# Two layers of memory attention and FNet on one core: rows of q and k by a direct transfer, a narrower memory update, and a new written order

## The chip, the core and the metric

The kernel runs on one core of a Trainium2 chip. The metric is the device time of one execution in microseconds. The core has five instruction streams that matter here: PE (matrix multiplies, with PEld for its weight loads), DVE, ACT and POOL (elementwise work), and SP (which issues the DMA transfers). PE's results land in PSUM; the other data lie in SBUF or DRAM.

## What is computed

The input x has 2048 rows of 512. Two layers are applied, each with an attention with memory (A) and a Fourier mixing (B); every step adds to a residual and starts from a layer norm without weights. Both layers use the same weights.

```python
# A, per head (H = 32 heads of 16), over N = 4 segments of L = 512 rows
for s in range(N):
    logits = einsum("bhqd,bhkd->bhqk", qs, ks) * scale + mask   # causal
    a_dot = softmax(logits) @ vs
    a_mem = (phi(qs) @ M) / (phi(qs) @ z + 1e-6)                # phi(t) = t+1 or exp(t)
    outs.append(g * a_mem + (1 - g) * a_dot)
    M = M + phi(ks)^T @ vs;  z = z + sum(phi(ks))
x = x + concat(outs) @ wo
# B
y = dft_seq_re @ (x @ dft_hid_re.T) - dft_seq_im @ (x @ dft_hid_im.T)
x = x + y
```

## The kernel before, in words

**Groups.** The attention is cut into 32 groups: two layers, four segments, and in each segment four groups of 8 heads. A group is numbered i. For each group `s_p` (line 784) projects q and k: the layer-normed rows stand transposed in a tile `g`, the weights in tiles `w`, both as a pair of 16-bit numbers (a high and a low part), so that each product is three matmuls `b<-g,w 128x512`. `t_split` (line 681) then splits the result in PSUM again into a high and a low half, in a tile that it calls `hl` (printed as `w`), and brings it to the row buffers `qst` and `kst`, in which the two halves lie on neighbouring partitions, so that one matmul of 48 rows gives the sum of three products. In the kernel before that goes by DRAM: two writes `d<-w` of 128 KB in all, and four reads `qst<-d` or `kst<-d`. There are two sets of row buffers (NR = 2), so the reads of group i wait until group i-2 has issued its last scores (the key `("ST", i-2)`).

**A group's way.** `s_x` (line 895) multiplies q rows by k rows (`b<-kst,qst`, 48 rows), DVE takes the causal row maxima (`junk<-b,cmask`, `mx`), and PE transposes them (`b<-identf,mx`). The maxima go as two more rows into `qst` (`qst<-mhl`), and `s_st` (line 946) makes the transposed scores with 50 rows (`b<-qst,kst`), the maximum subtracted already. ACT takes the exponential (`w<-b,fac`), POOL zeroes the part above the diagonal (the affine select), and `s_av` (line 969) multiplies by the values: `b<-w,vt`, four matmuls of 32 weight columns side by side, in 32-bit numbers, each of two passes. The 32 columns are 16 values and 16 ones, which give the softmax's sum. `s_mem` (line 838) multiplies phi(k) with the values (`b<-vt,w`, 192 columns, again two passes) and `t_merge` (line 651) joins both results. 24 of the 32 groups have a memory update, each of four matmuls, so 24 x 4 x 2 = 192 passes. `vt` is the tile of values; it is written by `t_v` (line 760) from PSUM.

**The layers' remaining work.** `s_o` (line 1028) multiplies by wo (`b<-wo,w`), adds the residual and norms again; `s_ab` (line 1145) multiplies by the hidden Fourier matrix (`b<-wd,w`); `s_r`, `s_c` and `s_f` load the sequence Fourier matrix in pieces, scale them and multiply (`b<-w,w 128x512`, the largest group of matmuls). All weights are scaled to powers of two first: maxima by DVE (`amax<-y`, `pmax<-y`), their sum over the partitions by PE (`b<-amax,ones`), scales by DVE (`gmax`, `scl`, `inv`, `fac`), and the split by ACT and DVE or POOL (`s_w`, line 440; `s_wo`, line 498, for wo and wd; the latter sets the key "WO", without which neither s_o nor s_ab starts). The weights are loaded into the tile `y`, which later holds the residual.

**What sets the order.** All engines run lists that are written out ahead. The parts above are generators; each `yield need(engine, tiles...)` stands for an instruction or a few, and a class Plan (line 50) keeps an estimate of when each engine and tile is free. At every step the generator goes on that could start first by that estimate; a table of offsets, LEAN (line 33), pulls or pushes single kinds. `t_warm` (line 1216) puts filler matmuls `b<-onesb` on PE where the estimate sees a gap. So a different estimate, offset or instruction moves much of the order. In the profile nearly every instruction has the line of one helper (L272 before, L280 in the changed kernel), so groups are told apart by their tiles.

**The start.** The first four row tiles of x are normed by `t_ln` with direct=True (line 585), transposed on PE (`b<-identh,w`), and copied to `g` by DVE or ACT; the statistics' small steps stand on POOL. Each group of the first segment waits for its own weights' scales.

Of the kernel before, what the change touches and what calls it, by code (L numbers as in the profile page):

```python
# [32 lines left out]
LEAN = dict(s_stT=150.0, s_memV=40.0, s_wV=80.0, s_rY=150.0, t_mergeA=40.0, s_xA=150.0, t_abA=40.0, t_mergeY=-150.0, s_mV=40.0, t_cV=-40.0, s_cA=-80.0, s_oY=40.0, t_cY=80.0, t_lnG=80.0, t_splitV=-40.0, t_phiA=150.0, s_kV=-300.0, t_mergeV=150.0, s_cT=80.0, s_avT=80.0, s_wA=-150.0, t_resV=-150.0, t_selG=40.0, s_lnY=-150.0, t_rowsY=300.0, t_ktY=-80.0)  # L33
# [9 lines left out]
PHM, EARLYLN, FEW = 5, 1, 0  # L43
WARM, IDLE, SPARE = 4200, 500.0, 300.0
DEEP = 1500.0
AHEAD = 2
NR = 2


class Plan:  # L50
# [31 lines left out]
    def key(self, a):  # L82
        f = self.fine.get(a.tensor.name)
        return (a.tensor.name, a.offset // f) if f else a.tensor.name
# [70 lines left out]
    def op(self, eng, name, args, kw):  # L155
# [19 lines left out]
        elif eng == "A":  # L175
            c = n / 1.2 + (52 if src else 93) + (93 if any(a.free_size() == 1 for a in ins) else 0)
        elif eng == "V":
# [9 lines left out]
        elif eng == "G":  # L187
            c = 127 + n * 0.915 if name == "affine_select" else 96 + n * 2.1
            if name == "tensor_tensor" and kw.get("op") == OP.pow:
                c = 300 + n * 165  # L190
            elif name == "partition_all_reduce":
                c = 370
# [86 lines left out]
def body(ctx: ExitStack, tc: tile.TileContext, x, wq, wk, wv, wo, beta, wd, cs, out):  # L279
# [61 lines left out]
    vt = [const.tile([128, TT, NP, 3, 16], F32, name=f"vt{i}") for i in range(NR)]  # L341
# [5 lines left out]
    bd = const.tile([128, 2, 4, 32], F32, name="bd")  # L347
# [65 lines left out]
    def share(o, src, s):  # L413
        yield need("A", src, s)
        A.activation(o[:, 0], src, AF.Copy, scale=s)
        A.activation(src, src, AF.Copy, scale=s)
        yield need("VG", o, src)
        tt(o[:, 1], src, o[:, 0], OP.subtract)

# [105 lines left out]
    def t_ones():  # L525
# [8 lines left out]
        for i in range(NR):  # L534
            for a in range(2):
                yield need("Y", d8, mode="b")
                Y.dma_start(kst[i][64 * a + 48:64 * a + 50].rearrange("r p n -> r (p n)"), d8, est=(415, 341, 472))
        done.add("KR")

    def s_k():  # L540
# [12 lines left out]
        for j in range(NR):  # L553
            V.memset(vt[j][:, :, :, 1, :], 1.0)
        done.add("VI")
        yield need("V")
        bits(rp, 3, 1.0)
        bits(ra, 64, 1.0 / 64)
        cj = sb("en", F32, (128, 2, 4, 32))
# [25 lines left out]
    def t_ln(src, xi, dst, key, direct=False):  # L585
        st = rg("bst", 2, F32, (128, 6))
        V.bn_stats(st, src)
        mv = rg("mv", 6, F32, (128, 4))
        V.bn_aggr(mv[:, 0:2], st)
        yield need("G", mv)  # L590
        rs = rg("rs", 6, F32, (128, 1))
        G.tensor_scalar(mv[:, 2:3], mv[:, 1:2], 1e-5, 2.0 ** -20, op0=OP.add, op1=OP.mult)
        G.tensor_tensor(rs, mv[:, 2:3], mhalf, op=OP.pow)
        G.tensor_scalar(mv[:, 3:4], mv[:, 0:1], rs, -1.0, op0=OP.mult, op1=OP.mult)
# [3 lines left out]
        if direct and pl.free["V"] < pl.free["A"]:  # L598
            yield need("V", xi)
            V.tensor_copy(hl[:, 0], xi)  # L600
        else:
            A.activation(hl[:, 0], xi, AF.Copy)
        yield need("VG", xi, hl)
        tt(hl[:, 1], xi, hl[:, 0], OP.subtract)
        pl.close(xi)
        if direct:
# [7 lines left out]
            if pl.free["A"] <= pl.free["V"]:  # L614
# [36 lines left out]
    def t_merge(e, o, gi, g, n, key):  # L651
# [8 lines left out]
        xa = x[:, 0]  # L660

        def view(off, *dims):
            return bass.AP(xa.tensor, xa.offset + off, [list(xa.ap[0])] + [list(d) for d in dims])

        yield need("V", x)
        d = view(16, (496, 2), (32, 16))
        if not gi:
            V.tensor_scalar(rc, d, 1e-6, None, op0=OP.add)
            d = rc
# [4 lines left out]
        for a in range(2):  # L674
            c = slice(16 * a, 16 * a + 16)
            tt(n.rearrange("p (b r) -> p b r", r=32)[:, :, c], view(528 * a, (32, 16), (1, 16)),
# [4 lines left out]
    def t_split(p, key, f, kphi):  # L681
# [10 lines left out]
        done.add(("half", key))  # L692
        yield need("Y", hl)
        d = tc.dram_tile([2, 2, 64, 512], F16)
        for a in range(2):
            Y.dma_start(d[a].rearrange("j p n -> p j n"), hl[64 * a:64 * a + 64], est=(651, 702, 467))
        i = key[1]
        if not kphi or q:
            pl.close(hl)
        elif i >= NR:  # L700
            spawn(t_kt(hl, kphi))
        if i >= NR:
            yield gate(("ST", i - NR))
        yield need("Y", d)
        order = key[0] == "dq"
        dst = (qst if order else kst)[i % NR]
        for a in range(2):
            f = d[a].rearrange("j (d p) n -> (j d) (p n)", p=NP)
            o = dst[64 * a:64 * a + 64].rearrange("r p n -> r (p n)")
            if order:  # L710
# [6 lines left out]
        if kphi and not q and i < NR:  # L717
            yield from t_kt(hl, kphi)
# [119 lines left out]
    def s_mem():  # L838
        for i in range(NGRP):
# [14 lines left out]
            if s < NSEG - 1:  # L854
# [10 lines left out]
                for a in range(2):  # L865
                    V.tensor_tensor(mu[:, a], mp[:, :, 16 * a:16 * a + 32], bd[:, a], op=OP.mult)
# [17 lines left out]
    def t_max(sp, mx, a, p0, w, t, left):  # L884
        n = 128 * (t + 1)
        for p in range(p0, p0 + w):
            o = (p - p0) * n
            yield need("V", sp)
            junk = rg("junk", 2, BF16)
# [5 lines left out]
    def s_x():  # L895
        for i in range(NGRP):
            yield gate(("dq", i), ("dk", i), "CM")
            qs, ks = qst[i % NR], kst[i % NR]
# [47 lines left out]
    def s_st():  # L946
        for i in range(NGRP):
            yield gate(("X", i), "KR")
            qs, ks = qst[i % NR], kst[i % NR]
# [378 lines left out]
```

## Time and profile before

| | |
|---|---|
| time, median of 3 runs | 1696.49 us (1695.97 to 1700.98) |
| the profiled execution | 1699.92 us, span 1698.2 us |
| mean granted clock | 0.989 |
| PE / DVE / ACT / POOL busy | 1662.3 / 1036.8 / 872.3 / 810.3 us |
| first projection, first maxima transposed | 16.88 us, 48.26 us |
| first matmul with wo | 171.61 us |
| PE waits on DVE's maxima | 10.6 us in 19 waits |

A row of a group reads: line, engine, operation, result<-operands, partitions x elements and type, xcount, then busy time, the mean of one, and the idle time of the engine just before with what ended it. PEld rows are weight loads; they may run beside PE. A row of windows has start:end, the length, then busy time and count for PE, PEld, DVE, ACT and POOL, the granted clock, the DMA share and GB/s. A row of the timeline is start, length, engine, operation, count.

### The profile page before, as it was taken

Reading aid. Unit: us, or ns where it says so; the run is one execution under the profiler, and the core shown is the slowest. Engines: PE = TensorE matmul, PEld = TensorE weight load, DVE = VectorE, ACT = ScalarE, POOL = GpSimd, SP = SyncE. Lnnn points to the kernel's source line nnn. Section 1 sums busy time; section 2 is a strip of 40 time slices with the busy share of each in tenths; the row PEclk is TensorE's granted clock in tenths of the full one; section 3 lists DMA queues with packets and bytes.
Section 4 is the critical chain, followed back from the end, with each engine's and each line's share of the span. In section 5 each row is a group of like instructions: output and inputs, shape, how many; then the busy total and the mean of one; then the engine's idle time right before and its main releaser. Section 6 shows DMA issues by size and latency. Waiting matters only on the chain.

```text
span 1698.2 us, 32247 instructions
## 1 busy us (share of the span) xinstructions
PE 1662.3 (98%) x11145; PEld 734.7 (43%) x11145; DVE 1036.8 (61%) x3262; ACT 872.3 (51%) x1480; POOL 810.3 (48%) x1445
## 2 busy tenths in 40 slices
PE   8889999999999999999999999999999999999999
PEld 4344344444444344444544444443444444444444
DVE  8784865778677786635768558546575765433221
ACT  5487577755656666535376754655455325312000
POOL 4376556575565556634255644635454415322000
PEclk9789999999999999999999999999999999999999
DMA  7546545655357432525746663543435322131423
GB/s 182 147 116 178 128 132 159 172 142 152 94 148 208 126 119 84 189 56 196 193 148 187 182 179 90 132 116 98 140 91 149 105 85 76 57 125 38 143 70 123
DMA packets 208629, 222.92 MB, mean 131 GB/s; under 512 B 104520, under 2 KB 127048, under 8 KB 208464
## 3 DMA queue, kind: packets, MB, share of 16 engines
q1 hardware_dynamic: 208464, 220.85, 45.8%
q8 instruction: 88, 1.44, 0.4%
q14 instruction: 77, 0.63, 0.1%
HBM read 137.40 MB, written 61.87 MB: 117 GB/s over the span
## 4 chain that ended last, share of the span: by engine, by line
PE 77%; DVE 9%; ACT 5%; issue 4%; DMA 3%; POOL 2%; SPq 1%; ACTq 0%; DVEq 0%; POOLq 0%
PE b L272 77%; ACT w L272 4%; DVE junk L272 4%; SPq L272 1%; DVE w L272 1%; POOL w L272 1%; DMA w<-w 1%; DMA w<-x 1%; DVE m L272 1%; DVE mx L272 1%; DVE y L272 1%; DVE bst L272 0%; DVE cam L272 0%; DMA w<-in_cs_dram 0%; DVE pmax L272 0%
## 5 line engine op out<-in xcount | busy, mean ns | idle before, releaser
L272 PEld LDWEIGHTS <-w 128*128 128x128 f16 x5056 | 467.8, 98 | 612.8 <-issue 101.1
L272 PE MATMUL b<-w,w 128*128 128x512 f16 x3072 | 708.5, 380 | 1.7 <-DVE mx L272 0.8
L272 ACT ACTIVATE w<-b,fac 128x512 f32<-128x512 f32 (+1 forms) x728 | 419.2, 655 | 176.3 <-PE b L272 175.8
L272 DVE CUSTOM_DVE_ANT_0 junk<-b,cmask 128x128 bf16<-128x128 f32 (+3 forms) x1024 | 436.3, 483 | 71.6 <-PE b L272 71.1
L272 POOL TENSOR_TENSOR w<-w,w 128x512 f16<-128x512 f32 (+1 forms) x294 | 347.5, 1187 | 247.1 <-ACT w L272 223.6
L272 POOL TENSOR_SCALAR_AFFINE_SELECT w<-w 128x128 f32<-128x128 f32 (+2 forms) x704 | 237.0, 350 | 202.7 <-ACT w L272 194.1
L272 DVE SCALAR_TENSOR_TENSOR y<-b,fyu,y 128x512 f32<-128x512 f32 x200 | 148.9, 745 | 235.6 <-PE b L272 235.2
L272 ACT ACTIVATE w<-w,csc 128x512 f16<-128x512 f32 (+1 forms) x256 | 180.1, 720 | 41.5 <-DVE csc L272 32.8
L272 PE MATMUL b<-g,w 128*128 128x512 f16 x768 | 183.1, 383 | 3.2 <-DMA g<-w 0.8
L272 PE MATMUL b<-wd,w 128*128 128x512 f16 x768 | 176.8, 379 | 0.1
L272 PE MATMUL b<-w,vt 128*32 128x512 f32 (+3 forms) x2048 | 172.4, 449 | 1.9 <-POOL w L272 1.1
L272 ACT ACTIVATE w<-b 128x512 f16<-128x512 f32 x128 | 75.9, 596 | 189.4 <-PE b L272 179.3
L272 DVE SCALAR_TENSOR_TENSOR w<-b,w 128x512 f16<-128x512 f32 x128 | 87.6, 687 | 120.3 <-ACT w L272 118.7
L272 ACT ACTIVATE w<-w 128x512 f16<-128x512 f32 (+1 forms) x137 | 86.5, 632 | 90.1 <-DVE w L272 87.9
L272 PE MATMUL b<-kst,qst 48*128 48x128 f16 (+3 forms) x1024 | 117.5, 304 | 6.3 <-DVE mx L272 3.2
L272 PE MATMUL b<-qst,kst 50*128 50x512 f16 (+3 forms) x1024 | 115.8, 302 | 5.5 <-DVE mx L272 2.2
L272 PE MATMUL b<-w,g 128*128 128x128 f16 x1536 | 96.3, 221 | 0.0
L272 PEld LDWEIGHTS <-g 128*128 128x128 f16 x1536 | 89.6, 99 | 12.7 <-issue 7.8
L272 DVE STREAM_TRANSPOSE m<-b 128x512 f32<-128x512 f32 x112 | 75.6, 698 | 31.1 <-PE b L272 30.7
L272 PEld LDWEIGHTS b<-w,vt 128*32 128x32 f32 x2048 | 54.8, 110 | 87.7 <-issue 48.2
L272 PE MATMUL b<-wo,w 128*128 128x512 f16 x384 | 89.1, 379 | 0.0
L272 PEld LDWEIGHTS <-kst 50*128 50x128 f16 x1024 | 37.3, 94 | 111.7 <-issue 105.2
(105 smaller groups left out, 1019.3 us busy)
## 6 DMA issues: line engine op xcount, KB each, us to landing
w<-in_cs_dram SPq DMA_DIRECT2D x128, 256.0 KB, 3.5
cc<-w SPq DMA_DIRECT2D x128, 256.0 KB, 3.2
w<-cc SPq DMA_DIRECT2D x128, 256.0 KB, 3.1
w<-w SPq DMA_DIRECT2D x96, 256.0 KB, 3.5
d<-w SPq DMA_DIRECT2D x128, 128.0 KB, 2.5
w<-in_x_dram SPq DMA_DIRECT2D x32, 256.0 KB, 3.6
qst<-d SPq DMA_DIRECT2D x64, 128.0 KB, 2.7
kst<-d SPq DMA_DIRECT2D x64, 128.0 KB, 3.3
```

Of the source, the lines that this page charges most:

```text
L272: r = f(*args, **kw)
```

## The change

1. **Direct transfer.** Where the row buffers are free when the split is made (by the order written out: the first three groups, and later ones whose earlier user has its scores issued), `t_split` sends `hl` to `qst` or `kst` in six transfers of 16x4x512 within SBUF. Elsewhere it goes by DRAM as before. Of the 64 q and k tiles 40 go directly and 24 by DRAM; SP issues 384 transfers for them in both kernels.
2. **A third row buffer** for group 2 alone, laid over rows 8 to 11 of `y`, which hold weights of the start; from group 3 on the two old ones alternate.
3. **Values.** `vt` is laid out with the head innermost: [128, TT, 32, 8], 16 values and 16 ones per head. The memory update takes 17 x 8 = 136 columns instead of 192. The weights of the value matmul are then 32 columns at a step of 8 numbers of 32 bits (before: next to each other). The columns of wv are put into the new order on the host, and `bd`, the mask of the products, becomes a 16-bit tile.
4. **Start.** For the first segment two of the three small steps of the layer norm's statistics go from POOL to DVE, and the low half `hl[:,1]` is always made on DVE. The other constants (`s_k`) wait for the scales of group 1. ACT copies to `g` only if it is free over 300 ns earlier than DVE.
5. **Order.** Ten entries of LEAN differ, the estimates of some durations on ACT and POOL too, and flags (YL, YB, YM, YC, YS) put further `yield need` between dependent instructions, so that others can come between. The fillers no longer wait for the key "CM".

```diff
-    vt = [const.tile([128, TT, NP, 3, 16], F32, name=f"vt{i}") for i in range(NR)]
+    kst.append(y[:, 8:10, :].bitcast(F16).rearrange("p a (b n) -> p (a b) n", n=512))
+    qst.append(y[:, 10:12, :].bitcast(F16).rearrange("p a (b n) -> p (a b) n", n=512))
+    ring = [0, 1, 2] + [(i - 3) % 2 for i in range(3, NGRP)]
+    prior = [None] * 3 + [0, 1] + list(range(3, NGRP - 2))
+    vt = [const.tile([128, TT, 32, HG], F32, name=f"vt{i}") for i in range(NR)]
...
+        yield gate(("F", 1))
...
+        if direct and STARTV:
+            yield need("V", mv)
+            V.tensor_scalar(mv[:, 2:3], mv[:, 1:2], 1e-5, 2.0 ** -20, op0=OP.add, op1=OP.mult)
+            yield need("G", mv)
+            G.tensor_tensor(rs, mv[:, 2:3], mhalf, op=OP.pow)
+            yield need("V", mv, rs)
+            V.tensor_scalar(mv[:, 3:4], mv[:, 0:1], rs, -1.0, op0=OP.mult, op1=OP.mult)
...
+        if direct:
+            yield need("V", xi, hl)
+            V.tensor_tensor(hl[:, 1], xi, hl[:, 0], op=OP.subtract)
...
+        i = key[1]
+        keep = kphi and not q
+        dst = (qst if q else kst)[ring[i]]
         yield need("Y", hl)
+        if i < DIRECT or prior[i] is not None and ("ST", prior[i]) in done:
+            if i == NR:
+                yield gate(*[("W", 2, g) for g in range(NG)])
+            for a in range(2):
+                o = dst[64 * a:64 * a + 64]
+                for r, j in ((0, 0), (16, 1), (32, 0)) if q else ((0, 0), (16, 0), (32, 1)):
+                    yield need("Y", hl)
+                    Y.dma_start(o[r:r + 16], hl[64 * a:64 * a + 64, j], est=(415, 520, 800))
+            done.add(key)
+            if keep:
+                yield from t_kt(hl, kphi)
+            else:
+                pl.close(hl)
+            return
...
+        if i > NR:
+            yield gate(("ST", prior[i]))
...
-        A.activation(vt[i % NR].rearrange("p t j e d -> p (t j) e d")[:, :, 0:3:2, :],
-                     p.rearrange("p t (j e d) -> p (t j) e d", j=NP, e=2), AF.Copy, scale=2.0 ** -24)
+        A.activation(vt[i % NR].rearrange("p t d h -> p t (d h)")[:, :, :128], p, AF.Copy, scale=2.0 ** -24)
...
-                mp = ps("pj", F32, (128, NP, 48))
+                mp = ps("pj", F32, (128, 17, HG))
                 for t in range(TT):
-                    T.matmul(mp, phk[:, 128 * t:128 * t + 128], v[:, t], start=(t == 0), stop=(t == TT - 1))
+                    T.matmul(mp, phk[:, 128 * t:128 * t + 128], v[:, t, :17], start=(t == 0), stop=(t == TT - 1))
                     yield need("T")
                 pl.close(phk)
                 yield need("V", mp, tag="mu" if s else ())
                 mu = macc[:, g] if s == 0 else sb("mu", F32, (128, 2, 4, 32))
-                for a in range(2):
-                    V.tensor_tensor(mu[:, a], mp[:, :, 16 * a:16 * a + 32], bd[:, a], op=OP.mult)
+                for e, d in ((0, HG), (16, 0)):
+                    V.tensor_tensor(view(mu, e, (128, 2), (32, NP), (1, 16)),
+                                    view(mp, HG * e, (NP, 2), (1, NP), (d, 16)),
+                                    view(bd, e, (128, 2), (32, NP), (1, 16)), op=OP.mult)
...
-                                 v[:, t, p].rearrange("k e d -> k (e d)")[:, 16 * a:16 * a + 32], tiles[p][1],
+                                 v[:, t, :, NP * a + p], tiles[p][1],
...
-        if "CM" not in done or at - pl.free["T"] < IDLE or pl.lately(at) >= WARM:
+        if at - pl.free["T"] < IDLE or pl.lately(at) >= WARM:
...
-        "wv": f["A_wv"],
+        "wv": f["A_wv"].reshape(D, NG, NP, 2, DH).transpose(0, 1, 4, 3, 2).reshape(D, D),
```

Of LEAN two of the entries that differ:

```diff
-t_lnG=80.0, t_abA=40.0
+t_lnG=-300.0, t_abA=150.0
```

**What moves at DVE's start.** The rows on DVE from the layer norm of the first tiles on; `w_85` to `w_91` are x tiles, `amax<-y` a maximum over weights, `g_277` the transposed tile. Before:

```order
L272 BN_AGGR mv<-bst 128x2
L272 CAST w_319<-w_85 128x512
L272 CAST w_329<-w_87 128x512
L272 TENSOR_REDUCE amax<-y 128x1 x2
L272 TENSOR_SCALAR gmax<-b_365 128x2
L272 TENSOR_SCALAR gmax<-gmax 128x2
L272 TENSOR_SCALAR scl<-gmax 128x2
L272 TENSOR_SCALAR inv<-gmax 128x2
L272 CAST w_344<-w_91 128x512
L272 COPY g_277<-b_404 128x8x128
```

The same engine in the changed kernel, at the last of the four x tiles:

```order
L280 TENSOR_REDUCE vm<-y 128x1 x4
L280 TENSOR_REDUCE amax<-vm 128x1
L280 TENSOR_TENSOR w_361<-w_89,w_361 128x512
L280 TENSOR_SCALAR mv<-mv,rs 128x1
L280 TENSOR_SCALAR gmax<-b_441 128x1
L280 TENSOR_SCALAR gmax<-gmax 128x1
L280 TENSOR_SCALAR scl<-gmax 128x1
L280 TENSOR_SCALAR inv<-gmax 128x1
L280 TENSOR_REDUCE amax<-y 128x1 x2
L280 CAST w_450<-w_91 128x512
L280 TENSOR_SCALAR gmax<-b_471 128x2
L280 TENSOR_SCALAR gmax<-gmax 128x2
```

The last x tile's layer norm stood behind the scales of one weight group; now it stands behind the maxima and scales of further groups and of all value weights, and each tile has a subtraction (`TENSOR_TENSOR`) and two small steps on DVE.

**What moves on SP.** The transfers behind the loads of the weights: `d<-w` writes a split tile to DRAM, `qst_106<-d` reads it, `qst_106<-w` is the direct one. Before:

```order
L272 DMA d<-w_490 64x2x512 x2
L272 DMA d<-w_507 64x2x512 x2
L272 DMA qst_106<-d 32x2048
L272 DMA qst_106<-d 16x2048
L272 DMA qst_106<-d 32x2048
L272 DMA qst_106<-d 16x2048
L272 DMA kst_104<-d 16x2048
```

After:

```order
L280 DMA qst_106<-w_562 16x4x512 x6
L280 DMA kst_104<-w_617 16x4x512 x6
L280 DMA_TRANSPOSE w_659<-w_617 128x8x128
L280 DMA y<-in_wo_dram 128x512 x2
L280 DMA qst_107<-w_673 16x4x512 x6
L280 DMA kst_105<-w_718 16x4x512 x6
L280 DMA_TRANSPOSE w_794<-w_718 128x8x128
```

Two writes and four reads per tile became six transfers in one step, with no read queued behind a write.

**What moves on PE at group 2's first scores.** `b_1459` and `b_1460` are PSUM tiles of scores. Before, with the old first row buffers (`qst_106`, `kst_104`), between scores of group 1:

```order
L272 LDWEIGHTS kst_105
L272 MATMUL b_1470<-qst_107,kst_105 128x384
L272 LDWEIGHTS kst_105
L272 MATMUL b_1471<-qst_107,kst_105 128x384
L272 LDWEIGHTS qst_106
L272 MATMUL b_1480<-kst_104,qst_106 128x128
```

After, from the third buffer, which prints as `y`:

```order
L280 LDWEIGHTS g_277
L280 MATMUL b_1389<-w_962,g_277 128x128
L280 LDWEIGHTS y
L280 MATMUL b_1459<-y 128x128
L280 LDWEIGHTS y
L280 MATMUL b_1460<-y 128x128
```

Before, group 2's first scores stand behind the first of group 1's transposed scores of 384 columns; now they stand ahead of all of these, and read a buffer that group 0 never used.

More of the change, by code (lines that the diff above doesn't have):

```diff
@@ L418, in share, with view @@
         tt(o[:, 1], src, o[:, 0], OP.subtract)
+    def view(t, off, *dims):
+        return bass.AP(t.tensor, t.offset + off, [list(t.ap[0])] + [list(d) for d in dims])
     def flat(t):
@@ L696, in t_split @@
             Y.dma_start(d[a].rearrange("j p n -> p j n"), hl[64 * a:64 * a + 64], est=(651, 702, 467))
-        i = key[1]
-        if not kphi or q:
+        if keep:
+            spawn(t_kt(hl, kphi))
+        else:
             pl.close(hl)
[L700 to L703, printed above, removed]
+        if i > NR:
+            yield gate(("ST", prior[i]))
         yield need("Y", d)
-        order = key[0] == "dq"
-        dst = (qst if order else kst)[i % NR]
         for a in range(2):
@@ L897, in s_x @@
             yield gate(("dq", i), ("dk", i), "CM")
-            qs, ks = qst[i % NR], kst[i % NR]
+            qs, ks = qst[ring[i]], kst[ring[i]]
             mx = rg("mx", 2, F32, (128, 2, NP, TT))
@@ L947, in s_st @@
         for i in range(NGRP):
-            yield gate(("X", i), "KR")
-            qs, ks = qst[i % NR], kst[i % NR]
+            yield gate(("X", i), ("KR", ring[i]))
+            qs, ks = qst[ring[i]], kst[ring[i]]
             kt = scores("t")
```

73 lines of the change are left out of this document (50 added, 23 removed).

## The prediction

> **What bounds the kernel now.** I read the page first, then the stages by windows, then PE's waits, then the start row by row.
>
> ```profile
> span 1698.2 us, 32247 instructions
> PE 1662.3 (98%) x11145; PEld 734.7 (43%) x11145; DVE 1036.8 (61%) x3262; ACT 872.3 (51%) x1480; POOL 810.3 (48%) x1445
> ```
>
> PE is busy for 98% of the span. The stages show where the other 2% lie:
>
> ```profile
> 0.00:49.00 49.00, 41.38 (x285) 20.60 (x286) 44.34 (x156) 24.19 (x37) 20.43 (x34) 1.00 0.76 194
> 55.00:159.00 104.00, 93.53 (x677) 38.07 (x674) 64.61 (x235) 84.48 (x149) 68.31 (x133) 0.84 0.48 128
> 159.00:187.00 28.00, 26.17 (x203) 12.86 (x201) 27.15 (x95) 13.31 (x22) 16.80 (x26) 1.00 0.64 169
> 187.00:1361.00 1174.00, 1161.96 (x8145) 514.11 (x8143) 776.70 (x2483) 684.88 (x1162) 641.41 (x1130) 1.00 0.50 140
> 1361.00:1698.00 337.00, 333.22 (x1803) 146.73 (x1803) 117.98 (x266) 64.17 (x111) 62.22 (x124) 1.00 0.28 88
> ```
>
> Up to 49 us DVE is the busy one (44.34 of 49, so 4.7 us idle), from 55 to 159 us ACT (84.48 of 104), from 159 to 187 us DVE again (27.15 of 28). Behind 187 us PE idles for 1174.00 - 1161.96 = 12.0 us and then 3.8 us, in all 1% of that time: there only less work on PE shortens the run. Ahead of it PE has slack, and what counts is when the last of the first four groups is done and the matmul with wo can begin.
>
> ```profile
> PE b L272 <- DVE mx L272: 10.6, 19, 1.6
> PE b L272 <- ACT w L272: 5.1, 13, 0.9
> PE b L272 <- POOL w L272: 3.0, 9, 0.8
> ...
> PE b L272 <- DMA g<-w: 0.8, 1, 0.8
> ...
> PE b L272 <- DMA qst<-mhl: 0.3, 1, 0.3
> ```
>
> These are PE's longest waits and all its waits on transfers. None is on `qst<-d` or `kst<-d`: the rows that the direct transfer speeds up are never late for PE by this view.
>
> **The change part by part.**
>
> *Memory update, 192 to 136 columns.* The price of a column comes from two rows of the same kind of product, 32 bits and two passes:
>
> ```profile
> L272 PE MATMUL b<-vt,w 128*128 128x192 f32 x192 | 38.6, 338 | 1.4 <-ACT vt L272 1.2 <-POOL w L272 0.2
> L272 PE MATMUL b<-w,vt 128*32 128x512 f32 x512 | 65.0, 620 | 0.5 <-ACT w L272 0.2 <-DVE mx L272 0.2
> L272 PE MATMUL b<-w,vt 128*32 128x128 f32 x512 | 21.4, 280 | 0.7 <-POOL w L272 0.5
> 10.35 0.30 PEld L272 LDWEIGHTS b<-amax,ones 128*128 128x128 f32 x2 [2.41 <-issue]
> ```
>
> (620 - 280) / 384 = 0.885 ns for a column, so 56 columns are 50 ns a pass. A pass of 136 columns is then 120 ns; the last row shows two loads of 128 x 128 numbers of 32 bits within 0.30 us, and as one lasts 0.19 us they start 0.11 us apart, so the load stays just under the pass and the gain is not cut off. Over 192 passes it is 9.5 us. The 32 passes of the first four groups lie where PE has slack; without them it is 160 x 50 ns = 7.9 us. I take **-8.5** (-7.9 to -9.5).
>
> *Start, up to wo.* The order shows what DVE does ahead of the first transposed maxima in addition: four subtractions `w<-w,w`, eight small steps `mv`, four `pmax`, one split `w<-b,w`, one copy to `g`, one cast, one `w<-w,fac`, two products with `bd`.
>
> ```profile
> L272 DVE TENSOR_TENSOR w<-w,w 128x512 f16<-128x512 f32 x2 | 2.1, 1062 | 5.8 <-ACT w L272 5.8
> L272 DVE TENSOR_REDUCE pmax<-y 128x1 f32<-128x512 f32 x12 | 7.6, 675 | 0.0
> L272 DVE SCALAR_TENSOR_TENSOR w<-b,w 128x512 f16<-128x512 f32 x128 | 87.6, 687 | 120.3 <-ACT w L272 118.7 <-POOL w L272 1.4
> L272 DVE COPY g<-b 128x1024 f16<-128x1024 f16 x2 | 1.4, 692 | 0.2 <-PE b L272 0.2
> L272 DVE CAST w<-w 128x512 f16<-128x512 f32 x7 | 4.4, 626 | 6.7 <-ACT w L272 6.7
> L272 DVE TENSOR_SCALAR w<-w,fac 128x512 f32<-128x512 f32 x24 | 12.7, 533 | 25.8 <-ACT w L272 25.8
> L272 DVE TENSOR_TENSOR macc<-b,bd 128x128 f32<-128x128 f32 x16 | 3.9, 283 | 5.8 <-PE b L272 5.8
> L272 DVE TENSOR_SCALAR rp<-rp 128x1 f32<-128x1 f32 x1 | 0.2, 154 | 0.0
> 16.88 1.46 PE L272 MATMUL b<-g,w 128*128 128x512 f16 x6 [0.68 <-ACT g L272]
> 34.39 0.62 PE L272 MATMUL b<-kst,qst 48*128 48x128 f16 x12
> 48.26 0.27 PE L272 MATMUL b<-identf,mx 128*32 128x128 f32 x1 [1.18 <-DVE mx L272]
> ...
> d<-w SPq DMA_DIRECT2D x128, 128.0 KB, 2.5
> ```
>
> 4 x 1.06 + 8 x 0.15 (by the step `rp`, the nearest of one column) + 4 x 0.68 + 0.69 + 0.69 + 0.63 + 0.53 + 2 x 0.28 = 11.3 us. (The subtractions bracketed lower, by the 0.69 of a split, leave 9.8.) DVE has 4.7 us idle there, and the direct rows, 2.5 us of writing less, may let it use some of that. So the first maxima, at 48.26 us before, come 5 to 11 us later; I take **+9**. The first projection (16.88) is late by most of it, since the last x tile's norm now stands behind the scales of more groups.
>
> Against it stands the third buffer. In the chain of waits group 2's rows have their place:
>
> ```profile
> 83.43 2.35 DMA qst<-d
> ...
> 90.67 0.42 PE L272 MATMUL b<-kst,qst 48*128 48x128 f16 x8
> 158.28 1.26 ACT L272 ACTIVATE w<-b,fac 128x512 f32<-128x512 f32 x2
> 171.61 5.35 PE L272 MATMUL b<-wo,w 128*128 128x512 f16 x24
> ```
>
> Group 2's rows were read at 83.43 us, behind group 0's last scores, its first scores ran at 90.67, and the last exponentials at 158.28. Without that gate group 2 can follow at once. From 55 to 159 us ACT idles for 104 - 84.48 = 19.5 us, which is the most that can come back; PE's clock of 0.84 there leaves it room too. Nothing in the trace says how much does, so the ends are 0 and -19.5, and I take the middle, **-9**: the exponentials still come in bursts behind the maxima.
>
> At the first wo PE then stands as before, but with less of the later work done ahead: by the order 12 matmuls `g,w` of 512 columns and 48 `w,g` of 128 are later than wo now.
>
> ```profile
> L272 PE MATMUL b<-g,w 128*128 128x512 f16 x768 | 183.1, 383 | 3.2 <-DMA g<-w 0.8 <-ACT w L272 0.7 <-ACT g L272 0.7
> L272 PE MATMUL b<-w,g 128*128 128x128 f16 x1536 | 96.3, 221 | 0.0
> 177.23 0.60 PE L272 MATMUL b<-onesb 128*128 128x512 bf16 x2
> 182.09 1.69 PE L272 MATMUL b<-onesb 128*128 128x512 bf16 x7
> 185.19 0.27 PE L272 MATMUL b<-identf,mx 128*32 128x128 f32 x1 [1.42 <-DVE mx L272]
> 185.30 0.81 PE L272 MATMUL b<-onesb 128*128 128x512 bf16 x3
> ```
>
> By busy time over count that is 12 x 0.238 + 48 x 0.063 = 5.9 us of work. Before, 12 fillers (3.1 us) and a wait (1.4 us) lay between wo and wd; the new order has no filler there. 5.9 - 4.5 = **+1.4**. The stage together: +9 - 9 + 1.4 = **+1.4** (5 - 19.5 + 1.4 = -13 to 11 + 1.4 = +12).
>
> *Values at a step of 8.* The load of 32 columns is in the trace only side by side:
>
> ```profile
> L272 PEld LDWEIGHTS b<-w,vt 128*32 128x32 f32 x2048 | 54.8, 110 | 87.7 <-issue 48.2 <-POOL w L272 23.4 <-DVE mx L272 3.0
> ```
>
> A load of 110 ns stands against a 128-column pass of 128 x 0.885 = 113 ns, so a longer load shows at once there, while the wider passes cover it. Four loads run together; 128 sets of four short passes and 123 first loads of a stretch are open, 251 in all. I take **0**: the load reads only 32 numbers. The upper end is its reading part twice as long: from 32 to 128 columns the load grows from 110 to 190 ns, 0.83 ns a column, so 32 columns are 27 ns, and 251 x 27 ns = +6.8; a gain has no reason.
>
> [...]
>
> *Behind 187 us.* Direct transfer: no wait of PE is on these rows, and SP issues six transfers either way; 0. Products with `bd`: 48 rows of 0.28 us on an engine with 397 us idle; even doubled they hide. One `junk` buffer instead of two: written and read by DVE alone; 0. The contiguous write of `vt` on ACT likewise. The new order can shift PE's 12.0 us of idle time both ways; I take **-2** (-6, half of it, to +8).
>
> **Sum.** 1699.9 - 8.5 + 1.4 + 0 - 2 = 1690.8 for the profiled execution. That run was 3.4 above the median of 1696.5, so on the median it is **1687.4**.
>
> **The rivals.** A measurement of this kernel tells about 0.3% (5.1 us) from no change.
>
> - *The forecast*, as summed: 1687. Chance 0.40, of it 0.36 faster and 0.04 the same.
> - *The third buffer returns all*: ACT's 19.5 us go. For: the chain has group 2's rows on it. Against: exponentials wait for maxima by DVE, which has more to do. wo comes 10.5 earlier: 1677. Chance 0.15, faster.
> - *The start's loss stays*: DVE was nearly full up to 49 us and again before wo, and the direct rows hide anyway since nothing on PE waited for them. 1687.4 + 9 to 11 = 1696 to 1698, and with the order's +8 and the rest some 1705. Chance 0.22: 0.14 the same, 0.08 slower.
> - *Slower by the strided load*: each value load of 32 columns becomes longer. For: the load has no slack beside the 128-column pass. Against: the reading part is only 27 of 110 ns. It crosses to slower when it costs 1701.6 - 1687.4 = 14.2 us, that is 57 ns over 251 loads; doubled in whole (110 ns) it costs 28 us: 1715. Chance 0.20, of it 0.09 the same, 0.11 slower. [...]
> - *The rest*: clock or order behind 187 us, slower, 0.03.
>
> **Range and chances.** Faster 0.36 + 0.15 = 0.51; the same 0.04 + 0.14 + 0.09 = 0.27; slower 0.08 + 0.11 + 0.03 = 0.22. The range goes from 1673 (full return, less the order's -4) to 1706 (start loss with a worse order; a good part of the strided case).
>
> **What would show it.** Right: a row `b<-vt,w 128x136` with 192 passes about 50 ns shorter; loads `b<-w,vt` still near 110 ns; first projection 5 to 12 us later than 16.88; first transposed maxima near 57; group 2's first scores well below 90.67 plus that delay; first wo at 171.6 or a little earlier; PE's idle time behind wo near 10 to 14 us. Wrong: loads `b<-w,vt` above 140 ns, wo behind 178 us, or PE's waits behind 187 us doubled.

## The result, and the profile after

| | before | changed |
|---|---|---|
| time, median | 1698.67 us (4 runs) | 1824.62 us (4 runs, 1822.41 to 1826.3) |
| span of the profiled execution | 1698.2 us | 1820.7 us |
| first projection / first maxima transposed | 16.9 / 48.3 us | 30.0 / 68.8 us |
| first matmul with wo | 171.6 us | 199.3 us |

The ratio is 1.074 (95% interval 1.0716 to 1.0766): 126 us slower, where 9 us faster was forecast and the range ended at 1706. The page of the changed kernel:

```profile
span 1820.7 us, 32400 instructions
PE 1710.0 (94%) x11160; PEld 751.9 (41%) x11160; DVE 1107.9 (61%) x3290; ACT 869.2 (48%) x1478; POOL 799.6 (44%) x1419
```

PE falls from 98% to 94%, and DVE, which has 28 instructions more, is busy 71 us longer. PE's waits say who is late:

```profile
PE b L280 <- DVE mx L280: 67.5, 130, 2.4
PE b L280 <- ACT w L280: 11.4, 20, 1.5
```

19 waits on the maxima (10.6 us) became 130 (67.5 us). The maxima's own groups on DVE, `junk` being the output that nobody reads, the widest before and then the changed kernel's:

```profile
L272 DVE CUSTOM_DVE_ANT_0 junk<-b,cmask 128x512 bf16<-128x512 f32 x256 | 162.2, 681 | 14.5 <-PE b L272 14.3
...
L280 DVE CUSTOM_DVE_ANT_0 junk<-b,cmask 128x512 bf16<-128x512 f32 x256 | 175.6, 686 | 55.1 <-PE b L280 29.4 <-DVE mx L280 0.5
...
L280 DVE CUSTOM_DVE_ANT_0 junk<-b,cmask 128x384 bf16<-128x384 f32 x256 | 141.9, 554 | 43.4 <-PE b L280 17.3
...
L280 DVE CUSTOM_DVE_ANT_0 junk<-b,cmask 128x256 bf16<-128x256 f32 x256 | 107.9, 421 | 27.4 <-PE b L280 8.8
```

One lasts as long as before (686 against 681 ns), but the 256 of the widest take 175.6 us of DVE instead of 162.2 (busy time counts an overlap once), and of the idle time ahead of them (55.1) only 29.4 has another engine behind it; the rest has no releaser of another engine. The timeline shows why. Before, maxima of 384 columns in a row:

```profile
40.27 0.08 DVE L272 DVE_READ_ACCUMULATOR2_ANT mx<- 128x1 f32 x1
40.27 0.55 DVE L272 CUSTOM_DVE_ANT_0 junk<-b,cmask 128x384 bf16<-128x384 f32 x1
40.75 0.08 DVE L272 DVE_READ_ACCUMULATOR2_ANT mx<- 128x1 f32 x1
40.75 0.55 DVE L272 CUSTOM_DVE_ANT_0 junk<-b,cmask 128x384 bf16<-128x384 f32 x1
```

The next maximum starts together with the read of the last result, and 0.07 us before the last one's record ends: 0.48 us from start to start. The changed kernel, maxima of 128 columns:

```profile
409.35 0.08 DVE L280 DVE_READ_ACCUMULATOR2_ANT mx<- 128x1 f32 x1
409.47 0.29 DVE L280 CUSTOM_DVE_ANT_0 junk<-b,cmask 128x128 bf16<-128x128 f32 x1
409.69 0.08 DVE L280 DVE_READ_ACCUMULATOR2_ANT mx<- 128x1 f32 x1
409.80 0.29 DVE L280 CUSTOM_DVE_ANT_0 junk<-b,cmask 128x128 bf16<-128x128 f32 x1
...
410.35 0.08 DVE L280 DVE_READ_ACCUMULATOR2_ANT mx<- 128x1 f32 x1
410.58 0.29 DVE L280 CUSTOM_DVE_ANT_0 junk<-b,cmask 128x128 bf16<-128x128 f32 x1
```

Now each starts 0.12 us behind the start of the read, and the last one shown 0.23 us. The median from start to start of two maxima of one width in a row, taken from the trace, goes from 212 to 334 ns (128 columns), 345 to 468 (256), 478 to 710 (384) and 611 to 844 (512). The larger steps are not a matter of width. By the semaphores in the trace, a maximum that waits for DVE's last one alone starts about 122 ns later than these medians of before (334 at 128 columns, 734 at 512); one that waits for a result of PE besides, like the one at 410.58, has a separate wait instruction in front and starts about 232 ns later (443 at 128 columns, 844 at 512). Most of the wide ones are of the second kind (170 of 177 at 384 columns, 157 of 164 at 512).

The loads of the values are longer too, and the memory update has its 136 columns:

```profile
L280 PEld LDWEIGHTS b<-w,vt 128*32 128x32 f32 x2048 | 67.5, 145 | 85.4 <-issue 50.6 <-POOL w L280 18.0 <-DVE mx L280 4.5
...
L280 PE MATMUL b<-vt,w 128*128 128x136 f32 x192 | 31.5, 308 | 4.3 <-DVE m L280 1.6 <-POOL w L280 1.4 <-ACT vt L280 0.8
```

### The profile page after: what moved, and what is told of

It reads as the page before. It is cut to its first block, busy times and chain, and to the rows that moved or that the text cites. A ratio compares the mean times of both kernels' runs of the same rounds, so it can differ in the third digit from the quotient of the medians.

```text
span 1820.7 us, 32400 instructions
## 1 busy us (share of the span) xinstructions
PE 1710.0 (94%) x11160; PEld 751.9 (41%) x11160; DVE 1107.9 (61%) x3290; ACT 869.2 (48%) x1478; POOL 799.6 (44%) x1419
## 4 chain that ended last, share of the span: by engine, by line
PE 66%; DVE 19%; issue 5%; DMA 3%; ACT 3%; POOL 2%; SPq 2%; DVEq 0%; ACTq 0%; POOLq 0%
PE b L280 66%; DVE junk L280 13%; ACT w L280 3%; DVE w L280 2%; SPq L280 2%; DMA w<-w 1%; POOL w L280 1%; DMA w<-in_cs_dram 1%; DVE cam L280 1%; DVE y L280 1%; DVE mx L280 1%; DVE m L280 1%; DMA w<-in_x_dram 1%; DVE bst L280 0%; DVEq L280 0%
## 5 line engine op out<-in xcount | busy, mean ns | idle before, releaser
L280 DVE CUSTOM_DVE_ANT_0 junk<-b,cmask 128x128 bf16<-128x128 f32 (+3 forms) x1024 | 499.3, 488 | 155.8 <-PE b L280 74.8
L280 ACT ACTIVATE w<-b,fac 128x512 f32<-128x512 f32 (+1 forms) x728 | 423.7, 654 | 240.1 <-PE b L280 237.4
L280 POOL TENSOR_TENSOR w<-w,w 128x512 f16<-128x512 f32 (+1 forms) x285 | 336.2, 1188 | 221.1 <-ACT w L280 210.4
L280 ACT ACTIVATE w<-w,csc 128x512 f16<-128x512 f32 (+1 forms) x256 | 173.9, 720 | 29.3 <-DVE csc L280 25.4
L280 PE MATMUL b<-w,vt 128*32 128x512 f32 (+3 forms) x2048 | 176.7, 463 | 3.8 <-DVE w L280 1.1
L280 PE MATMUL b<-qst,kst 50*128 50x512 f16 (+1 forms) x992 | 129.1, 305 | 39.1 <-DVE mx L280 30.4
L280 PE MATMUL b<-kst,qst 48*128 48x128 f16 (+1 forms) x992 | 123.2, 308 | 17.9 <-DVE mx L280 14.2
L280 PEld LDWEIGHTS b<-w,vt 128*32 128x32 f32 x2048 | 67.5, 145 | 85.4 <-issue 50.6
L280 DVE TENSOR_REDUCE cam<-w 128x1 bf16<-128x512 f32 x128 | 82.0, 676 | 14.6 <-DMA w<-in_cs_dram 14.5
```

What stands on the lines that cost most here:

```text
L280: r = f(*args, **kw)
```

## The experiments

Each time is a median beside runs of the kernel before on the same chip; where an edit could move the order, the planner's counts were held so that it did not, unless the text says otherwise.

**The discarded output.** The theory: with one `junk` buffer each maximum waits on its own engine for the one before. The rival: order, start and value loads cost the time.

```diff
-            junk = rg("junk", 1, BF16)
+            junk = rg("junk", 2, BF16)
-            mhl = rg("mhl", 2, F16, (32, 2, 128))
+            mhl = rg("mhl", 1, F16, (32, 2, 128))
-        rc = rg("rc", 4, F32, (128, 2, 16))
+        rc = rg("rc", 1, F32, (128, 2, 16))
```

> The changed kernel with two buffers again for the maxima's discarded output (junk); every engine's order is unchanged; the place is paid for by one buffer instead of two for mhl and one instead of four for rc. Theory J (each maximum on DVE waits for the one before it since both write the same junk buffer): the idle time before the junk rows falls by about 80 us, PE's waits on DVE's maxima go from 67 us back to 10 to 20, and the time falls by 110 to 135 us from the changed kernel's 1824.6, to 1690 to 1715. Rival O (the new order, the late start and the longer value loads cost the time, the maxima wait only because PE is late): under 30 us come back, 1795 or more.

Measured: 1720.7 us (ratio to before 1.0153, 1.014 to 1.0166), 104 us less than the changed kernel. Its maxima:

```profile
L280 DVE CUSTOM_DVE_ANT_0 junk<-b,cmask 128x512 bf16<-128x512 f32 x256 | 162.7, 681 | 33.9 <-PE b L280 33.7
...
L280 DVE CUSTOM_DVE_ANT_0 junk<-b,cmask 128x256 bf16<-128x256 f32 x256 | 92.2, 418 | 13.2 <-PE b L280 13.2
```

The idle time without a releaser is gone (33.7 of the 33.9 us have PE behind them), and the 256 of the widest take 162.7 us of DVE again (162.2 before). The time came out 6 us above the range expected. PE's waits on the maxima are back at the size of before:

```profile
PE b L280 <- DVE mx L280: 8.9, 20, 2.1
```

The 104 us include whatever the smaller `mhl` and `rc` cost; the next run has no such addition. The other way round, in the kernel before:

```diff
-            junk = rg("junk", 2, BF16)
+            junk = rg("junk", 1, BF16)
```

> The kernel before with one junk buffer instead of two, nothing else; the order is unchanged. Theory J: 1024 maxima, each about 0.11 us later behind the one before, add 100 to 140 us: 1800 to 1840. Rival O: within 15 us of 1698.7.

Measured: 1812.1 us (1.0687, 1.0671 to 1.0702), 117 us more from one number.

```profile
PE b L272 <- DVE mx L272: 68.5, 124, 3.3
```

PE's named waits on the maxima grow by 58 us; PE's busy time grows by another 49 (1662.3 to 1711.4), 31.7 of it in the eight rows of the scores, whose matmuls stand further apart (256 of 512 columns, `b<-kst,qst`, take 54.7 us instead of 47.6 at a mean of 403 instead of 396 ns). The largest part of the loss is shown from both sides. How the number came into the change is not shown; the space fits it: the new `vt` takes 32 x 8 instead of 4 x 48 numbers for each of four tiles, 1 KB more in each of two buffers, and a `junk` buffer holds 1 KB.

**The values.** The changed kernel with two `junk` buffers, but the old layout; the 136 columns are picked out of the 192 (the neighbouring column of ones serves both heads):

```diff
-    vt = [const.tile([128, TT, 32, HG], F32, name=f"vt{i}") for i in range(NR)]
+    vt = [const.tile([128, TT, NP, 3, 16], F32, name=f"vt{i}") for i in range(NR)]
...
-                    T.matmul(mp, phk[:, 128 * t:128 * t + 128], v[:, t, :17], ...)
+                    T.matmul(mp, phk[:, 128 * t:128 * t + 128], view(v[:, t], 0, (48, NP), (31, 2), (1, 17)), ...)
...
-                                 v[:, t, :, NP * a + p], tiles[p][1],
+                                 v[:, t, p].rearrange("k e d -> k (e d)")[:, 16 * a:16 * a + 32], tiles[p][1],
```

> The changed kernel with two junk buffers and the old layout of the values: the value loads read 32 neighbouring columns again, and the memory update takes its 136 columns out of the 192 by a pattern of three steps; every engine's order is unchanged. Theory S (a load at a step of 8 is 145 instead of 110 ns and is open in 251 places): 251 x 35 ns = 9 us less than the changed kernel with two junk buffers, loads back at 110 ns. Rival (the longer load hides beside the passes): within 3 us of it.

Measured: 1714.9 us (1.012, 1.0107 to 1.0133), 5.8 us below the run with the strided loads (which also has smaller `mhl` and `rc`), with

```profile
L280 PEld LDWEIGHTS b<-w,vt 128*32 128x32 f32 x2048 | 53.6, 110 | 89.0 <-issue 51.3 <-POOL w L280 19.7 <-DVE mx L280 5.1
```

110 ns a load against 144 (the run with the strided loads). 34 ns x 251 open places is 8.5 us; two thirds of it is what the time shows, though the passes of the memory update stand 124 instead of 116 ns apart in this run, which over 192 passes takes 1.5 us from the difference. The same cut in the kernel before, its order held:

```diff
-                mp = ps("pj", F32, (128, NP, 48))
+                mp = ps("pj", F32, (128, NP, 2, 17))
...
-                    T.matmul(mp, phk[:, 128 * t:128 * t + 128], v[:, t], ...)
+                    T.matmul(mp, phk[:, 128 * t:128 * t + 128], view(v[:, t], 0, (48, NP), (31, 2), (1, 17)), ...)
```

> The kernel before, with only the memory update cut to 136 of the 192 columns by a pattern of three steps; the order is unchanged. By the term of the prediction: 7.9 to 9.5 us less than before, about 1690. Rival (the load of the 128 columns bounds the pass, or the strided pattern slows the pass): within 3 us of before.

Measured: 1692.3 us against 1695.3 (0.9984, 0.9974 to 0.9993), the only kernel of this study that is faster than before, by 3.0 us where 7.9 to 9.5 were expected. The rival's number came, but not by its reason: the passes did become shorter.

```profile
L272 PE MATMUL b<-vt,w 128*128 128x136 f32 x192 | 31.0, 299 | 1.2 <-ACT vt L272 1.0 <-POOL w L272 0.2
```

Against 38.6 us before, PE saves 7.6 us in this row; the passes stand 123 instead of 163 ns apart (116 in the changed kernel, whose columns are neighbours). Less than half of it comes out as time: PE idles 2.2 us more behind wo, and what lies ahead of wo is covered.

**The direct transfer.** What is left of the loss is 1714.9 against 1695.3. First the direct transfer alone, in the kernel before, with an order that the planner wrote anew:

```diff
+        if i < NR or ("ST", i - NR) in done:
+            for a in range(2):
+                o = dst[64 * a:64 * a + 64]
+                for r, j in ((0, 0), (16, 1), (32, 0)) if q else ((0, 0), (16, 0), (32, 1)):
+                    Y.dma_start(o[r:r + 16], hl[64 * a:64 * a + 64, j], est=(415, 520, 800))
+            done.add(key)
```

> The kernel before with the direct transfer alone: 34 of the 64 tiles of q and k go from the split tile to the row buffers within SBUF, with the two old buffers; offsets, estimates, start and values are those of before, and the planner writes the order out anew with them. Theory O (what is left of the loss comes from the new order and the start, the direct transfer is hidden): within 5 us of before's 1695. Theory D (six issues of about 0.62 us hold SP longer than two and four): 8 to 20 us slower. Forecast's view (nothing waits on these rows behind the start): 0 to -5.

Measured: 1729.4 us (1.0194, 1.0166 to 1.0222), 35 us slower, which is more than either theory allowed. With the third buffer, whose declarations are those of the change:

```diff
+    ring = [0, 1, 2] + [(i - 3) % 2 for i in range(3, NGRP)]
+    prior = [None] * 3 + [0, 1] + list(range(3, NGRP - 2))
```

> The same with the third row buffer for group 2 as well; 36 tiles go directly. Theory O: within 5 us of the run with two buffers, with the first matmul of wo earlier by 0 to 10 us, since group 2 no longer waits for group 0; 1686 to 1698. Theory D: 1703 or more.

Measured: 1718.7 us (1.0135, 1.0109 to 1.0162); the first wo came at 177.7 instead of 184.0 us, so the buffer seems to return time, as far as two different orders can be compared. The other way, the changed kernel (two `junk` buffers, old values) without direct transfers:

```diff
-        if i < DIRECT or prior[i] is not None and ("ST", prior[i]) in done:
...
-    ring = [0, 1, 2] + [(i - 3) % 2 for i in range(3, NGRP)]
+    ring = [i % NR for i in range(NGRP)]
```

> The changed kernel with two junk buffers and the old values (1714.9), but all rows of q and k by DRAM through two buffers as before; the offsets, estimates and the start of the change stay, the order is written out anew. Theory O: 1707 to 1722, the loss stays. Theory D: 1705 or less. The first transposed maxima come at 67 us or later.

Measured: 1717.3 us (1.0118, 1.0088 to 1.0148). The first wo stands at 195.3 us there, 17 later than with the direct transfer and the third buffer, and only 2.4 us of that show at the end: the new order also has PE do more ahead of wo (busy for 167 us there, against 147). So the transfer seems to cost 35 us in one place and nothing in the other, but each of these runs has an order of its own. That was taken away next: in the kernel before, 36 tiles go directly at the place where their writes stood, while the planner goes on counting two writes and four reads; PE, DVE, ACT and POOL run exactly the old lists.

```diff
+        straight = i < NR or ("ST", i - NR) in done
+        if straight:
+            for a in range(2):
+                for r, j in ((0, 0), (16, 1), (32, 0)) if order else ((0, 0), (16, 0), (32, 1)):
+                    nc.sync.dma_start(dst[64 * a:64 * a + 64][r:r + 16], hl[64 * a:64 * a + 64, j])
```

> The kernel before with 36 of the 64 tiles of q and k sent directly at the place where their two writes stood, and the order of PE, DVE, ACT and POOL left exactly as it was (the planner still counts the way by DRAM). Theory O (the direct transfer is hidden, the 35 us of its run with a new order came from the order): within 4 us of before's 1695. Theory D (direct transfers themselves cost, six issues of about 0.62 us on SP and 64 KB pieces): 10 to 35 us slower.

Measured: 1734.1 us (1.0224, 1.02 to 1.0248). The theory that it is hidden fell. As both kernels run the same lists, the traces can be laid side by side, matmul by matmul: the lag grows in a dozen jumps, one of 4.3 us at 285 us. SP there, before (a timeline; the transposed k tile is DMA_TRANSPOSE):

```profile
268.94 2.73 SPq L272 DMA_DIRECT2D d<-w  x4
271.76 1.31 SPq L272 DMA_TRANSPOSE w<-w  x1
...
274.63 1.77 SPq L272 DMA_DIRECT2D qst<-d  x4
276.44 2.04 SPq L272 DMA_DIRECT2D kst<-d  x4
```

and with direct transfers in the same order:

```profile
270.35 3.86 SPq L703 DMA_DIRECT2D qst<-w  x6
274.31 3.75 SPq L703 DMA_DIRECT2D kst<-w  x6
278.50 1.29 SPq L272 DMA_TRANSPOSE w<-w  x1
```

The twelve issues for q and k take 3.86 and 3.75 us, where the four writes for both took 2.73 and the reads came behind the transpose. So the transpose starts 6.7 us later (278.50 against 271.76), 5 beyond the lag of 1.4 us there. ACT before, then ACT and PE in that run:

```profile
276.34 0.72 ACT L272 ACTIVATE w<-w,fac 128x512 f32<-128x512 f32 x1
...
284.02 0.72 ACT L272 ACTIVATE w<-w,fac 128x512 f32<-128x512 f32 x1 [6.36 <-issue]
284.65 0.58 ACT L272 ACTIVATE vt<-b 128x512 f32<-128x512 f32 x1
...
285.27 0.48 PE L272 MATMUL b<-qst,kst 50*128 50x384 f16 x1 [3.97 <-ACT vt L272]
```

ACT stands 6.36 us at phi(k), which needs the transposed tile, and the copy for which PE then waits is queued behind it. In both traces the transposed tile lands 0.87 us ahead of phi(k), at 275.47 and at 283.15 us. No wait of PE in that run is on the rows themselves. Whether this is the cause, or the transfer within SBUF, four runs tell. Four more small issues, no direct transfer:

```diff
+        if i < NR or ("ST", i - NR) in done:
+            for a in range(2):
+                for j in range(2):
+                    more = tc.dram_tile([16, 512], F16)
+                    nc.sync.dma_start(more, hl[64 * a:64 * a + 16, j])
```

> The kernel before with all rows by DRAM, but with four more small transfers (16 rows of 1 KB into a DRAM tile that nobody reads) behind the two writes of the 36 tiles that the run with the old order sent directly; every engine's order is that of before. Theory Q (six issues stand on SP where two stood, 3.8 us instead of about 1.5, and what is queued behind them, the transpose of k above all, is late): 20 to 45 us slower than before. Theory R (the transfer itself, SBUF to SBUF, is what costs): within 8 us of before.

Measured: 1755.1 us (1.0352, 1.0337 to 1.0368): issues alone do it, and more than expected. With the reads there are ten issues for each of these tiles, and here PE does wait for rows (`kst<-d`, 3.8 us). Then 17 k tiles directly, behind their transpose or ahead of it:

```diff
         Y.dma_start(kt.rearrange(...), hl.rearrange("p j n -> p (j n)"), transpose=True)
+        send()
         pl.close(hl)
```

> The order of before, with 17 k tiles sent directly, each behind its own transpose on SP (or where its reads stood, if that is earlier); q by DRAM. Theory Q: within 6 us of before, 1690 to 1702. Theory R: 12 to 20 us slower.

Measured: 1696.4 us (1.0003, 0.999 to 1.0016). For the other place, against the run with 36 tiles:

```diff
-        straight = i < NR or ("ST", i - NR) in done
+        straight = not q and kphi and i >= NR and ("ST", i - NR) in done
```

> The same 17 k tiles sent directly, but ahead of their transpose, where the two writes stood. Theory Q: 10 to 25 us slower than before, and slower than with the transpose first by 8 or more. Theory R: as with the transpose first.

Measured: 1715.0 us (1.0112, 1.009 to 1.0134). The same 17 tiles, the same transfers: nothing behind the transpose, 18 us ahead of it. In the old order the cost of the k tiles' direct transfer is SP's issue time in front of the transpose. The other 20 of the 38 us of the run with 36 tiles belong to the 15 q tiles and four other k tiles, which no run has alone; at 270 us the six issues for q stand ahead of the transpose too. And in the changed kernel's order (two `junk` buffers, old values), the k tiles' transfers put behind the transpose by the same `send`:

> The changed kernel with two junk buffers and the old values (1714.9), its order held, but the direct transfers of a k tile put behind its transpose. Theory Q: 5 to 15 us faster, 1700 to 1710. Rival (in the new order the planner has counted the six issues, so that nothing waits for the transpose): within 4 us of 1714.9.

Measured: 1718.0 us (1.0135, 1.011 to 1.016), no gain over 1714.9. That is the rival's result; its reason, that the planner had counted the six issues and spread what waits for the transpose, is not shown.

**Start and order.** The changed kernel (two `junk` buffers, old values) with the start of before (two of the flags for the order, YL and YB, are off as well, and the order is written anew):

```diff
-STARTV, YL, YB, YM, YC, YS = 1, 1, 1, 1, 1, 1
+STARTV, YL, YB, YM, YC, YS = 0, 0, 0, 1, 1, 1
...
-        yield gate(("F", 1))
...
-t_lnG=-300.0
+t_lnG=80.0
```

> The changed kernel with two junk buffers and the old values (1714.9), but with the start of before: the layer norm's small steps on POOL, the subtraction on DVE or POOL, the constants not held back, the offset of the norm's POOL steps 80 again, the fillers behind the masks. Direct transfer and third buffer stay. Theory St (the start's delay of 18.7 us to the first maxima is what is left): first maxima back near 46 to 50, wo at 166 to 172, and the time falls by 7 to 15 us, to 1700 to 1708. Rival (the order behind the start): within 4 us of 1714.9.

Measured: 1721.3 us (1.0153, 1.0131 to 1.0175). The first maxima did come earlier, at 52.6 instead of 67.0 us, and yet wo stood at 179.2 and the time did not fall. An earlier first maximum alone gained nothing; as wo did not come back to 166 to 172, the run does not tell what an earlier wo would be worth. Three runs of the kernel before ask what an order alone is worth. One offset moved:

```diff
-s_cT=80.0
+s_cT=90.0
```

> The kernel before with one offset of the planner's table changed from 80 to 90 (PE's steps of s_c), nothing else: the same instructions in another order. Theory O (the table was fitted to one order, and any new order without a fit loses some 20 us): 1705 to 1730. Rival (orders by this planner lie close together, and what costs is in the parts of the change): within 5 us of 1695.

Measured: 1703.5 us (1.0047, 1.003 to 1.0064), between the two. The 136 columns with an order written anew, against the run with the order held:

```diff
-            n, w = (192 if out[0].free_size() == 136 else out[0].free_size()), aps[1]
+            n, w = out[0].free_size(), aps[1]
```

> The kernel before with 136 columns in the memory update (1692.3 with the order held), this time with the planner counting 136, so that it writes a new order. Theory O: 1705 to 1730. Rival: within 5 us of 1692.

Measured: 1725.2 us (1.0173, 1.0138 to 1.0209), 33 us above the same work in the old order. And the changed kernel's offsets alone:

```diff
-LEAN = dict(... t_lnG=80.0, t_abA=40.0 ...)
+LEAN = dict(... t_lnG=-300.0, t_abA=150.0 ...)
```

> The kernel before with the changed kernel's table of offsets alone. Theory O: 1705 to 1735, since the table fits neither. Rival (the new table is no worse): within 5 us of 1695.

Measured: 1724.7 us (1.0166, 1.0144 to 1.0188). Orders that this planner wrote anew cost 8 to 30 us with almost the same instructions. The 19.6 us that the changed kernel keeps with two `junk` buffers and the old values lie inside that spread.

## Why the prediction was wrong, point by point

**The step that failed** stands under the part behind 187 us: "One `junk` buffer instead of two: written and read by DVE alone; 0." That DVE alone uses it was the reason given for no cost, and is the reason for the cost: with two buffers the next maximum starts 0.07 us ahead of the last one's end, with one it waits on its own engine and starts 0.04 to 0.16 us behind it. It cost 104 us in the changed kernel and 117 in the old one. The list of the change ahead of the prediction does not name this number at all. A warning stood in the trace: starts that are 0.48 us apart while a record lasts 0.55 show that the records overlap, and 1024 of them lie on the way to PE. The overlap alone, 0.07 us x 1024 = 72 us, would still have been too little: it leaves out those 0.04 to 0.16 us a maximum. No rival named it, so the range could not hold the time.

**Memory update**, -8.5: PE's row fell by 7.6 us with the old layout, as worked out; the time by 3.0. The mechanism is right, the step from PE's work to the end is not: part of it turned into waits.

The start of the changed kernel with two `junk` buffers, in rows of its timeline (the last copy to `g` on DVE, the first maxima's transpose, the first wo):

```profile
28.97 0.68 DVE L280 COPY g<-b 128x1024 f16<-128x1024 f16 x1
...
66.99 0.27 PE L280 MATMUL b<-identf,mx 128*32 128x128 f32 x1 [0.44 <-DVE mx L280]
...
178.28 4.05 PE L280 MATMUL b<-wo,w 128*128 128x512 f16 x18
```

**Start**, +9 to the first maxima and -9 by the third buffer: the first maxima came 18.7 us later (67.0 against 48.3, two `junk` buffers). The rows counted on DVE were right, but the price came from one engine, and the start is a chain over several: the first projection alone is 13 us late, as the last x tile's norm waits at every step for its turn behind the scales. With the old start it stands at 16.5 us again. Most of the delay comes back, since wo is 6.7 us late (178.3): the return is 12 us, where 9 was taken. How much of it is the third buffer's is not isolated: it was 6 us in the old kernel, and 17 together with the direct transfer in the changed one, each time between two different orders.

What the start costs at the end is seen in windows ahead of the first wo and behind it, before and in the changed kernel with two `junk` buffers and the old values:

```profile
0.00:171.61 171.61, 153.22 (x1134) 68.23 (x1134) 127.29 (x476) 114.06 (x193) 97.61 (x181) 0.90 0.58 154
171.61:1698.21 1526.60, 1509.04 (x10013) 666.49 (x10011) 909.49 (x2789) 758.21 (x1287) 712.72 (x1265) 1.00 0.45 129
...
0.00:178.17 178.17, 147.09 (x1089) 63.94 (x1090) 132.03 (x502) 110.36 (x188) 88.64 (x166) 0.91 0.47 132
178.17:1711.95 1533.78, 1511.91 (x10071) 666.27 (x10070) 910.26 (x2789) 753.18 (x1290) 708.41 (x1254) 1.00 0.43 123
```

PE idles 171.61 - 153.22 = 18.4 us ahead of wo before and 31.1 there, and behind wo 17.6 and 21.9. So 13 of the 17 us that PE idles more lie at the start. The prediction's count of PE's work that is later than wo now, 5.9 us, fits (153.2 - 147.1 = 6.1 us); that the start would keep a loss of about this size was one of its rivals, with a chance of 0.22.

**Value loads**, 0 with +6.8 as the end: +5.8, at 34 ns a load where 27 was the bound. The loads took 110 ns with neighbouring columns and 144 at a step of 8. Why the step costs this is not shown; the doubling that gave the bound was the author's estimate from the loads of 32 and 128 columns (110 and 190 ns).

**Direct transfer**, 0 since SP issues six either way: the count was right and the place was not weighed. In the old order six in one go cost 38 us over 36 tiles, 18 of them by the 17 k tiles ahead of their transposes; in the changed order the runs tell no cost. That no wait of PE names these rows said nothing of what is queued behind them on SP.

**Order**, -2 (-6 to +8): the size was wrong. Some 20 us are left in the changed kernel, the start's loss included; runs of other orders give 8 to 30.

All three signs that the prediction had named for being wrong came: loads of 145 ns, a first wo at 199.3 us (178.3 with two `junk` buffers), and PE's idle time behind wo more than doubled (17.6 to 72 us). The last is the work of `junk`: with two buffers it is 25 us.

**What stays open**: which part of the changed order costs these 20 us. Neither the start, nor the direct transfers, nor their place ahead of the transpose brought them back one at a time, and the first two of these runs have new orders of their own. That the old table fits one order closely, so that any other is worse, is argued from three orders, not shown.

## What to carry to other kernels

An output that nobody reads still has a writer: before a buffer for it is cut to one, look in the timeline whether its writers overlap, and whether others wait for their results; here the overlap multiplied by their count was 72 us, and the one buffer cost 104 and 117. Price a transfer by its issue time and by what stands behind it on its queue, not by whether its own data are waited for: the same 17 direct transfers of k cost 18 us ahead of the transposes and nothing behind them. Where a planner writes the order, hold the order while one thing is changed; a run with a new order measures both (8 to 30 us here for the order).

## What the runs showed of the hardware

- DVE, waiting on its own engine for the last maximum (changed kernel against the one before): about 122 ns more from start to start, and about 232 where the maximum also waits for PE, at 128 columns (334 and 443 ns against 212) as at 512 (734 and 844 against 611). Each of these maxima has an accumulator read of 0.08 us behind it.
- A direct transfer of 64 KB within SBUF held SP for 0.62 to 0.64 us (3.75 and 3.86 for six, the run with 36 tiles in the old order), a read of 64 or 128 KB from DRAM for 0.44 to 0.51 (1.77 and 2.04 for four, before).
- A load of 32 weight columns of 32 bits at a step of 8 took 144 ns (changed kernel with two `junk` buffers; 145 with one), of neighbouring ones 110 (before, and with the old values).
- A pattern of 17 columns at a time made a pass of 136 columns 123 ns long (the kernel before with 136 columns), against 116 for neighbouring columns (changed kernel).
